# A new order and a new choice of engines for attention followed by a max-of-three feed-forward layer, on one Trainium2 core

## The chip, the core and the metric

The kernel runs on one core of one Trainium2 chip. Its engines are TensorE (PE in the profile; its weight loads are PEld), VectorE (DVE), ScalarE (ACT), GpSimd (POOL) and SyncE (SP). They run side by side, each through its own list of instructions in order, and wait for one another through semaphores. The metric is device time in microseconds: 200.65 us is the median of three runs before the change (200.58 to 200.71). The profile is of one execution with a span of 199.3 us.

## The reference

Batch 4, 8 heads, 768 positions, head size 64. Heads of one kind ("retrieval") see the whole past; the others see the first 4 positions and a window of 64. The attention output, 3072 rows of 512, goes through three projections whose elementwise maximum goes through a fourth.

```python
def _attn_ref(q, k, v, is_retrieval, n_sink, window):
    scores = scale * np.matmul(q, k.transpose(0, 1, 3, 2))
    stream_keep = causal & (is_sink | in_win)
    mask = np.where(retr[0, :, 0, 0, None, None], full_mask, stream_mask)
    scores = np.where(mask[None], scores, -1000000000.0)
    a = np.exp(scores - np.max(scores, axis=-1, keepdims=True))
    a = a / (np.sum(a, axis=-1, keepdims=True) + 1e-09)
    return np.matmul(a, v).astype(np.float32)

def _moe_ref(x, w1, w2, w3, w_out):          # x: 3072 x 512, w1..w3: 512 x 768, w_out: 768 x 512
    h = np.maximum(np.maximum(x @ w1, x @ w2), x @ w3)
    return (h @ w_out).astype(np.float32)
```

## The kernel before

The work is cut into 16 tasks t: batch (4), half of the sequence (2), group of four heads (2). A task has two pairs of heads, i = 0 and 1, and its scores come in units u: two for the first half of the sequence, four for the second. For each unit TensorE makes the scores in PSUM (`st`), ScalarE takes the exponential into `pt` in SBUF, and a mask is multiplied in place. That multiply is on GpSimd unless (t, i, u) stands in a list:

```python
    MASK_ON_DVE = ((2, 0, 1), (3, 0, 0), (3, 0, 1), (3, 1, 3), (5, 0, 0), (5, 1, 0), (5, 1, 1), (7, 0, 1))

    def masks(t, i, u):
        # ...
        for at, u0, nu, cols, n, m0 in APART if t in (3,) else MASKED[half]:
            # ... x: a part of pt, m: the mask of the two heads
            engine = nc.vector if (t, i, u) in MASK_ON_DVE else nc.gpsimd
            engine.tensor_tensor(out=x, in0=x, in1=m, op=ALU.mult)
```

`APART` cuts one 512-element mask of task 3 into two of 256 elements. In task 0 and 1 the masks are added in PSUM by TensorE instead (from `mk`, built by `head_masks`).

V is cast from fp32 to fp16 (`va`), and a second copy `vf` is multiplied by a flag for each head (zero where a head doesn't see far keys). The engine of each is an argument:

```python
    def prep_v(t, i, op, vf_engine):
        # ...
        op(out=vdst, in_=vs[:, hs])                        # the cast into va
        vf_engine.tensor_tensor(out=vf[...], in0=..., in1=far[...], op=ALU.mult)
```

`av(t, i)` multiplies `pt` with `va` and `vf` on TensorE (`oacc`); VectorE takes the reciprocal of the row sums (`rc`) and scales (`x`). `x` is transposed into `xT`, for tasks 0, 1 and 3 by TensorE (`turn_x`, written `x t i` in the table below), for the others by a DMA. When all four pairs of a half are there, the feed-forward `ffn` of that half joins a queue: 18 groups of four matmuls (`yy`), moved from PSUM by ScalarE (`acc`) and VectorE (the maximum, into `acc` and `hT`), and 6 output matmuls for each of three row blocks. `fill(n)` takes n steps from that queue, so that TensorE has work between scores.

Q and K of batch 0 come as fp32, are cast (`cast_pair`: `kn`, `qn`), transposed by TensorE (`turn_pair`) and copied to `KQ`. Those of batches 1 to 3 are loaded by a casting DMA of GpSimd's queue (`load`, tile `kq`) and transposed by VectorE (`turn`, a 32 x 32 STREAM_TRANSPOSE into `KQ`).

The opening is a hand-written sequence of such calls, the rest a table with a row for each unit of scores: the number of queue steps, whether the two pairs are apart, and four places for calls (ahead of the scores, after them, half-way through the queue steps, at the end). In it `v 2 0 ap` is `prep_v` for task 2, pair 0, cast on ScalarE (a), `vf` on GpSimd (p); d is VectorE.

```python
    cast_pair(0, 0, (act, act))
    idle_work(8)                 # matmuls on zeros
    read_flags()
    idle_work(2)
    head_flags()
    turn_pair(0, 0, dve, act)
    head_masks(0, True)
    cast_pair(0, 1, (pool, act))
    turn_pair(0, 1, dve)
    # ...
    FIRST = 4                    # units 0 to 3 (tasks 0 and 1) are in the opening
    PROGRAM = (
        (2.4, True, "", "", "cast 1 2 dp", ""),
        (2.4, False, "load 1 0", "", "cast 1 3 da", ""),
        # ... 45 more rows
    )
    for (units, apart, *lines), slot in itertools.zip_longest(PROGRAM, SLOTS[FIRST:]):
        run(lines[0])
        if slot and apart:
            scores(*slot, (0,)); part = int(due + units / 3); fill(part); due -= part; scores(*slot, (1,))
        elif slot:
            scores(*slot)
        run(lines[1])
        due += units
        part = int(due / 2); fill(part); due -= part
        run(lines[2])
        part = int(due); fill(part); due -= part
        run(lines[3])
```

PSUM's eight banks: four in the pool `bank` (feed-forward, `oacc`, transposes), and two buffers of two banks for scores.

Of the kernel before, what the change touches and what calls it, by code (L numbers as in the profile page):

```python
# [34 lines left out]
    [(0, 0, 1, (0,), 256, 256), (0, 0, 1, (384,), 128, 0), (1, 1, 1, (0,), 256, 0)],  # L35
    [(1, 0, 2, (384,), 128, 0), (2, 2, 1, (0, 384), 128, 128), (3, 3, 1, (0,), 256, 0)],
]

APART = [(0, 0, 1, (384,), 128, 0), (1, 1, 1, (384,), 128, 0)] + MASKED[1][1:]


def _where(half):
# [9 lines left out]
def kernel(  # L52
# [14 lines left out]
    nc = tc.nc  # L67
# [50 lines left out]
    cast = {}  # L118
# [16 lines left out]
    def cast_pair(half, hp, engines):  # L135
        cast[half, hp] = []
        for nm, src, op in zip(("kn", "qn"), staged.pop((half, hp)), engines):
            x = half16.tile([P, HB, 2, D], FP16, tag=nm, name=nm)
            op(out=x, in_=src.rearrange("p h j d -> p j h d"))  # L139
            cast[half, hp].append(x)  # L140
# [84 lines left out]
    def idle_work(n):  # L225
        sink = sps.tile([P, 2, 512], FP32, tag="st", name="st")
        for _ in range(n):
            nc.tensor.matmul(sink[:, 0, :], zero[:, 0:P], zero, start=True, stop=True)
# [41 lines left out]
    def read_flags():  # L270
        nc.vector.tensor_scalar(
            out=RT1, in0=ir32[:, 0 : 2 * H : 2], scalar1=0.0, scalar2=None,
            op0=ALU.not_equal,
        )

    def head_flags():
        flags = bank([P, H], FP32, "flags")
        nc.tensor.matmul(flags, base[0:1, 0:P], RT1, start=True, stop=True)
        nc.vector.tensor_copy(out=RT, in_=flags)
        nc.vector.tensor_scalar(  # L280
            out=least, in0=RT, scalar1=-1.0, scalar2=1.5, op0=ALU.mult, op1=ALU.add
        )
# [10 lines left out]
    def head_masks(hp, early=False):  # L293
        for h in (2 * hp, 2 * hp + 1):
            nc.vector.tensor_scalar(
                out=mk[:, h], in0=kept, scalar1=least[:, h : h + 1],
                scalar2=-30000.0 if early else None,
                op0=ALU.is_le if early else ALU.is_gt,
                **({"op1": ALU.mult} if early else {}),
            )  # L300
# [4 lines left out]
    def load_weight(wi):  # L305
        if wi < 3:
            nc.gpsimd.dma_start(
                out=w_t[wi],
                in_=(moe_w1, moe_w2, moe_w3)[wi].rearrange("(ks p) n -> p ks n", p=P),
            )  # L310
        else:
            nc.gpsimd.dma_start(
                out=woutt, in_=moe_w_out.rearrange("(ns p) m -> p ns m", p=P)
            )
# [62 lines left out]
    def fill(n):  # L377
        while n > 0 and queue:
            try:
                next(queue[0])  # L380
                n -= 1
            except StopIteration:
                queue.pop(0)
# [73 lines left out]
                masks(t, i, u)  # L457


    MASK_ON_DVE = ((2, 0, 1), (3, 0, 0), (3, 0, 1), (3, 1, 3), (5, 0, 0), (5, 1, 0), (5, 1, 1), (7, 0, 1))  # L460

    def masks(t, i, u):
        b, half, qd = where(t)
        pt = pts[t, i]
        h0 = 4 * qd + 2 * i
        for at, u0, nu, cols, n, m0 in APART if t in (3,) else MASKED[half]:
            if at != u:
                continue
            m = mk[:, h0 : h0 + 2, m0 : m0 + n]
            if nu == 1 and len(cols) == 1:  # L470
                x = pt[:, u0, :, cols[0] : cols[0] + n]
            elif nu == 2:
                x = pt[:, u0 : u0 + 2, :, cols[0] : cols[0] + n]
                m = m.unsqueeze(1).to_broadcast([P, 2, 2, n])
            else:
                x = pt[:, u0].rearrange("p h (c n) -> p h c n", n=n)[:, :, 0:4:3]
                m = m.unsqueeze(2).to_broadcast([P, 2, 2, n])
            engine = nc.vector if (t, i, u) in MASK_ON_DVE else nc.gpsimd
            engine.tensor_tensor(out=x, in0=x, in1=m, op=ALU.mult)  # L479
# [40 lines left out]
    def turn_x(t, i, op=None):  # L520
# [18 lines left out]
    cast_pair(0, 0, (act, act))  # L539
    idle_work(8)  # L540
    read_flags()
    idle_work(2)
    head_flags()
    turn_pair(0, 0, dve, act)
    head_masks(0, True)
    cast_pair(0, 1, (pool, act))
    turn_pair(0, 1, dve)
    cast_pair(0, 2, (pool, pool))
    scores(0, 0, (0,))
    scores(0, 1, (0,))  # L550
    head_masks(1, True)
    load_weight(0)
    scores(0, 0, (1,))
    far_flags()
    cast_pair(0, 3, (pool, pool))
    head_masks(3, True)
    head_masks(2, True)
    turn_pair(0, 2, dve)
    scores(0, 1, (1,))
    turn_pair(0, 3, dve)  # L560
    prep_v(0, 0, dve, nc.gpsimd)
    prep_v(1, 0, dve, nc.vector)
    load_pairs(1, 0, 2, (nc.gpsimd, nc.gpsimd))
    prep_v(1, 1, pool, nc.gpsimd)
    scores(1, 0, (0,))
    scores(1, 1, (0,))
    scores(1, 0, (1,))
    prep_v(0, 1, act, nc.vector)
    av(0, 0)
    scores(1, 1, (1,))  # L570
    av(1, 0)
# [1 line left out]
    turn_x(0, 0, act)  # L573
    av(1, 1)
    load_weight(1)
    turn_x(0, 1, act)
    head_masks(0)
    cast_pair(1, 1, (act, act))
    load_pairs(1, 2, 2, (nc.gpsimd, nc.gpsimd))
    load_weight(2)  # L580
    load_v(0, 1, (nc.gpsimd,) * HB)
    turn_x(1, 0, dve)
    turn_x(1, 1, dve)
    cast_pair(1, 0, (act, act))
    fill(4)
    head_masks(2)
    turn_pair(1, 1, dve)
    turn_pair(1, 0, dve)
    head_masks(3)
    load_weight(3)  # L590
    fill(1)
    fill(1)
    fill(1)
    head_masks(1)
# [5 lines left out]

    FIRST = 4
    PROGRAM = (
        (2.4, True, "", "", "cast 1 2 dp", ""),
        (2.4, False, "load 1 0", "", "cast 1 3 da", ""),
        (2.0, False, "", "pair 1 2", "load 1 1", ""),
        (2.2, False, "pair 1 3", "v 2 0 ap", "", "v 2 1 ap"),
        (2.2, False, "", "gate, load_v 1 0", "", ""),
        (1.6, True, "", "av 2 0", "", "turn 1 0 0 0"),
        (1.0, True, "turn 1 0 0 1", "", "av 2 1, turn 1 0 1 0", ""),
        (2.2, True, "turn 1 0 1 1, load_v 1 1", "", "v 3 1 pp, v 3 0 ap, x 2 0", "turn 1 1 0 0"),  # L610
        (3.6, False, "turn 1 1 0 1", "x 2 1", "turn 1 1 1 1, av 3 1", ""),
        (2.8, False, "v 4 0 pp, av 3 0", "turn 1 1 1 0", "v 4 1 ap", ""),
        (3.6, False, "x 3 0, x 3 1", "", "", ""),
        (3.6, False, "av 4 0", "", "x 4 0, v 5 1 pp", "x 4 1, v 5 0 ap"),
        (2.8, False, "", "", "av 4 1", "av 5 0, load 2 0, v 6 0 pp"),
        (3.6, False, "x 5 0", "load 2 1", "", "av 5 1"),
        (3.8, False, "", "x 5 1", "", ""),
        (2.8, False, "", "load_v 2 0", "turn 2 0 1 0", "v 6 1 ap"),
        (4.8, False, "turn 2 0 0 1", "", "turn 2 0 0 0", "av 6 0"),
        (4.2, False, "", "", "", "x 6 0, x 6 1, turn 2 0 1 1"),  # L620
        (3.4, False, "", "av 6 1", "turn 2 1 0 1", ""),
        (5.4, False, "load_v 2 1", "v 7 0 ap, turn 2 1 0 0", "turn 2 1 1 0", "v 7 1 ap"),
        (3.4, False, "", "turn 2 1 1 1", "v 8 0 ap, x 7 0", "av 7 0"),
        (3.8, False, "av 7 1", "", "", "v 8 1 pp"),
        (3.94, False, "x 7 1", "", "av 8 0", "v 9 0 ap, av 8 1"),
        (3.2, False, "", "x 8 0, x 8 1", "", ""),
        (3.94, False, "", "", "av 9 0, v 9 1 ap", "load 3 0"),
        (3.6, False, "", "x 9 0, load 3 1", "x 9 1", ""),
        (5.6, False, "v 10 0 ap, av 9 1", "v 10 1 ap", "", ""),
        (3.14, False, "", "load_v 3 0", "turn 3 0 1 0", ""),  # L630
        (3.6, False, "turn 3 0 0 1", "av 10 0", "turn 3 0 0 0", ""),
        (3.4, False, "", "x 10 0", "av 10 1", "turn 3 0 1 1"),
        (6.2, False, "", "", "turn 3 1 0 1", "v 11 0 ap"),
        (3.2, False, "load_v 3 1", "turn 3 1 0 0", "turn 3 1 1 0", ""),
        (3.2, False, "v 11 1 pp", "x 10 1, turn 3 1 1 1", "v 12 0 ap", "av 11 0, x 11 0"),
        (3.4, False, "", "av 11 1", "", "v 12 1 ap"),
        (5.0, False, "x 11 1", "", "av 12 0", "v 13 0 ap, av 12 1"),
        (3.2, False, "", "x 12 0, x 12 1", "", ""),
        (4.0, False, "", "", "av 13 0, v 13 1 pp", ""),
        (5.2, False, "", "x 13 0", "x 13 1", ""),  # L640
        (3.94, False, "v 14 0 ap, av 13 1", "v 14 1 ap", "", ""),
        (4.4, False, "", "", "", ""),
        (4.0, False, "", "av 14 0", "", ""),
        (3.2, False, "", "x 14 0", "av 14 1", ""),
        (3.2, False, "", "", "", "v 15 0 ap"),
        (4.6, False, "", "", "", ""),
        (3.94, False, "v 15 1 ap", "x 14 1", "", "av 15 0, x 15 0"),
        (3.94, False, "", "av 15 1", "", ""),
        (3.94, False, "x 15 1", "", "", ""),
    )  # L650
    ops = {"d": dve, "a": act, "p": pool}
    engines = {"d": nc.vector, "p": nc.gpsimd}
# [2 lines left out]
        av=lambda *a: av(*map(int, a)),  # L655
# [71 lines left out]
```

The softmax here doesn't subtract the row's maximum and nothing guards it: scores larger than these inputs give would overflow.

## Time and profile before

| what | value |
|---|---|
| time, median of 3 | 200.65 us |
| profiled span | 199.3 us |
| PE busy | 189.7 us, 95% |
| DVE busy | 122.5 us, 61% |
| ACT busy | 131.7 us, 66% |
| POOL busy | 123.3 us, 62% |
| DMA moved | 26.48 MB, mean 133 GB/s |

Busy time is the union of an engine's instructions; in the groups of instructions the last numbers are total, mean of one in ns, and the idle time of the engine just ahead of them with what ended it. Several instructions start before the one ahead has ended by the record, so busy time in a short stretch can be less than the sum of durations. DMA is a share of 16 engines and passes 1 where records overlap. The chain is followed back from the last instruction through whatever released each step. Numbers of lines in a profile, L479 and so on, are those of the kernel's file.

### The profile page before, as it was taken

The page shows a single profiled execution, that of the slowest core. Times are in us where ns is not written, and L with a number is a line of the kernel's source. Part 1 is how long each engine was busy: PE and PEld are TensorE (multiplying, and loading weights), DVE is VectorE, ACT ScalarE, POOL GpSimd, SP SyncE. Part 2 cuts the span into 40 slices and gives each one's busy share as a digit, 9 for nine tenths or more (in the row PEclk, how much of TensorE's full clock was granted, in tenths as well). Part 3 has the DMA queues.
Part 4 walks back from the last instruction along what each step waited for, and adds up shares of the span by engine and source line. Part 5 has one row for each costly group of instructions (what it writes and reads, how often), then busy time and mean ns, then how long its engine had stood idle before and what let it go on. Part 6 is the DMA issues. An engine that isn't in the chain of part 4 may idle for free.

```text
span 199.3 us, 5133 instructions
## 1 busy us (share of the span) xinstructions
PE 189.7 (95%) x2059; PEld 109.5 (55%) x2059; DVE 122.5 (61%) x241; ACT 131.7 (66%) x206; POOL 123.3 (62%) x154
## 2 busy tenths in 40 slices
PE   7897999996999999999999999999999999999992
PEld 2455555545566465574555565565555565755652
DVE  2698587999687829861555649961555234543540
ACT  4585798786966776676786775848758769323221
POOL 3599159789887906787969635799847447400000
PEclk9999999999999999999999999999999999999999
DMA  6999999994949991904359995513410250023004
GB/s 182 270 213 245 278 238 212 213 202 112 256 81 154 194 274 43 178 0 146 95 101 132 170 254 141 85 26 98 116 23 20 105 76 20 3 64 135 3 0 158
DMA packets 43245, 26.48 MB, mean 133 GB/s; under 512 B 33558, under 2 KB 38230, under 8 KB 43222
## 3 DMA queue, kind: packets, MB, share of 16 engines
q1 hardware_dynamic: 37206, 15.01, 34.9%
q0 software_dynamic: 4784, 10.23, 26.7%
q10 hardware_dynamic: 1232, 0.92, 1.5%
q8 instruction: 16, 0.26, 0.6%
q14 instruction: 7, 0.06, 0.1%
HBM read 25.17 MB, written 6.29 MB: 158 GB/s over the span
## 4 chain that ended last, share of the span: by engine, by line
PE 78%; DVE 8%; ACT 4%; DMA 3%; issue 3%; POOL 2%; SPq 1%; ACTq 0%; POOLq 0%; DVEq 0%
PE yy L338 43%; PE yy L364 12%; PE st L441 10%; PE oacc L495 8%; DVE KQ L190 4%; PE yst L338 3%; ACT pt L452 3%; DMA ks<-in_k_dram 2%; DVE x L505 2%; DMA out_dram<-ot 1%; PE tr L157 1%; PE yst L364 1%; POOL kn L139 1%; DVE hT L349 1%; POOL qn L139 0%
## 5 line engine op out<-in xcount | busy, mean ns | idle before, releaser
L479 POOL TENSOR_TENSOR pt<-pt,mk 128x512 f16<-128x512 f16 (+1 forms) x76 | 80.6, 1084 | 34.8 <-ACT pt L452 34.7
L452 ACT ACTIVATE pt<-st 128x1024 f16<-128x1024 f32 (+3 forms) x99 | 83.1, 894 | 19.4 <-PE st L441 18.6
L349 DVE TENSOR_TENSOR acc<-yy,acc 128x384 f16<-128x384 f32 x45 | 25.1, 558 | 28.9 <-PE yy L338 19.3
L338 PE MATMUL yy<-xT,w1t 128*128 128x384 f16 x180 | 36.1, 327 | 0.1
L338 PE MATMUL yy<-xT,w0t 128*128 128x384 f16 x180 | 35.6, 326 | 0.4 <-DVE xT L531 0.4
L338 PE MATMUL yy<-xT,w2t 128*128 128x384 f16 x180 | 35.7, 327 | 0.0
L346 ACT CAST acc<-yy 128x384 f16<-128x384 f32 x45 | 21.0, 485 | 17.0 <-PE yy L338 10.5
L364 PE MATMUL yy<-woutt,hT 128*128 128x512 f16 (+1 forms) x138 | 32.0, 375 | 0.0
L441 PE MATMUL st<-KQ 32*128 32x384 f16 (+4 forms) x560 | 28.7, 279 | 1.0 <-DVE KQ L190 0.8
L349 DVE TENSOR_TENSOR hT<-yy,acc 128x384 f16<-128x384 f32 x45 | 25.1, 560 | 6.6 <-PE yy L338 4.0
L495 PEld LDWEIGHTS <-pt 128*128 128x128 f16 x672 | 24.0, 97 | 5.3 <-issue 2.1
L190 DVE STREAM_TRANSPOSE KQ<-kq 128x384 f32<-128x384 f32 x24 | 25.7, 1130 | 0.0
L338 PEld LDWEIGHTS <-w0t 128*128 128x128 f16 x192 | 18.2, 98 | 12.9 <-issue 1.0
L495 PE MATMUL oacc<-va,pt 128*128 128x65 f16 x352 | 24.8, 193 | 0.3 <-ACT va L392 0.3
L338 PEld LDWEIGHTS <-w2t 128*128 128x128 f16 x192 | 17.6, 98 | 13.3 <-issue 2.1
L338 PEld LDWEIGHTS <-w1t 128*128 128x128 f16 x192 | 17.2, 98 | 12.8 <-issue 1.3
L370 ACT COPY ot<-yy 128x512 f32<-128x512 f32 x22 | 12.9, 588 | 15.9 <-PE yy L364 9.6
L364 PEld LDWEIGHTS <-hT 128*128 128x128 f16 x150 | 14.0, 98 | 14.6 <-issue 0.3
L441 PEld LDWEIGHTS <-KQ 32*128 32x128 f16 (+1 forms) x560 | 12.2, 93 | 17.8 <-issue 11.5
L495 PE MATMUL oacc<-vf,pt 128*128 128x65 f16 x320 | 21.2, 193 | 0.8 <-POOL vf L394 0.8
L505 DVE TENSOR_TENSOR x<-oacc,rc 128x384 f16<-128x384 f32 x32 | 17.8, 557 | 1.1
L503 DVE RECIPROCAL rc<-oacc 128x6 f32<-128x6 f32 x32 | 6.1, 192 | 20.0 <-PE oacc L495 19.8
(70 smaller groups left out, 129.9 us busy)
## 6 DMA issues: line engine op xcount, KB each, us to landing
out_dram<-ot SPq DMA_DIRECT2D x23, 256.0 KB, 3.1
vs<-in_v_dram SPq DMA_DIRECT2D x21, 256.0 KB, 6.3
kq<-in_k_dram POOLq DMA_DIRECT2D x6, 384.0 KB, 5.6
kq<-in_q_dram POOLq DMA_DIRECT2D x6, 384.0 KB, 8.0
qs<-in_q_dram ACTq DMA_DIRECT2D x4, 192.0 KB, 4.0
ks<-in_k_dram SPq DMA_DIRECT2D x4, 192.0 KB, 3.6
w0t<-in_moe_w_dram POOLq DMA_DIRECT2D x1, 768.0 KB, 7.4
ks<-in_k_dram POOLq DMA_DIRECT2D x2, 384.0 KB, 7.2
```

The source lines that it names most:

```text
L190: nc.vector.transpose(out=dst.rearrange("c (p j) -> c j p", j=n)[:, j0:j1], in_=src.rearrange("c (j i) -> c j i", i=R),)
L338: nc.tensor.matmul(yy[:, 0:HALF], w_t[wi][:, ks, ni * P : (ni + 1) * P], xT[b, half][ks].rearrange("p a t -> p (a t)"), start=(ks == 0), s ...
L346: nc.scalar.copy(out=acc[ni], in_=yy[:, 0:HALF])
L349: nc.vector.tensor_tensor(out=dst, in0=yy[:, 0:HALF], in1=acc[ni], op=ALU.max)
L364: nc.tensor.matmul(yo[:, 0:n], hT[ns][:, tb * P : (tb + 1) * P], woutt[:, ns, c : c + n], start=(ns == 0), stop=(ns == NNB - 1),)
L370: op(out=ot[:, c : c + n], in_=yo[:, 0:n])
L441: nc.tensor.matmul(sts[g // m][:, g % m, c0 : c0 + n * P], KQ[rows, 0, ki * P : (ki + 1) * P], KQ[rows, 1, t0 : t0 + n * P], start=(c0 == ...
L452: nc.scalar.activation(out=pts[t, i][:, u, h0 : h0 + m, 0:w], in_=st[:, :, 0:w], func=AF.Exp, scale=sc,)
L479: engine.tensor_tensor(out=x, in0=x, in1=m, op=ALU.mult)
L495: nc.tensor.matmul(o[:, qi, hl, 0 : D + 1], pt[:, u, hl, c : c + P], vv[:, 2 * hp + hl, ki, 0 : D + 1], start=(idx == 0), stop=(idx == len ...
L503: nc.vector.reciprocal(out=rc, in_=o[:, :, :, D])
L505: nc.vector.tensor_tensor(out=x, in0=o[:, :, :, 0:D], in1=rc.unsqueeze(3).to_broadcast([P, HB, 2, D]), op=ALU.mult,)
```

## The change

The table and the opening's order were set anew by an offline search, together with the engines that do the masks and the V casts. Its stated aim is to keep VectorE's casts from running beside GpSimd's work. The computation is the same. `APART` goes; the list of masks on VectorE goes from 8 entries to 14, without (3, 0, 0). Cut to the core:

```diff
-APART = [(0, 0, 1, (384,), 128, 0), (1, 1, 1, (384,), 128, 0)] + MASKED[1][1:]
-    MASK_ON_DVE = ((2, 0, 1), (3, 0, 0), (3, 0, 1), (3, 1, 3), (5, 0, 0), (5, 1, 0), (5, 1, 1), (7, 0, 1))
+    MASK_ON_DVE = ((2, 0, 1), (2, 0, 3), (3, 0, 1), (3, 1, 3), (5, 0, 0), (5, 1, 0), (5, 1, 1), (7, 0, 1), (9, 0, 0), (11, 0, 1), (11, 0, 2), (13, 0, 0), (15, 0, 1), (15, 0, 2))
-        for at, u0, nu, cols, n, m0 in APART if t in (3,) else MASKED[half]:
+        for at, u0, nu, cols, n, m0 in MASKED[half]:
     read_flags()
+    head_flags()
+    cast_pair(0, 1, (pool, act))
     idle_work(2)
-    head_flags()
+    head_masks(0, True)
     turn_pair(0, 0, dve, act)
-    head_masks(0, True)
-    cast_pair(0, 1, (pool, act))
     turn_pair(0, 1, dve)
 # ... cut
     turn_pair(0, 2, dve)
+    turn_pair(0, 3, dve)
     scores(0, 1, (1,))
-    turn_pair(0, 3, dve)
 # ... cut
     turn_x(0, 1, act)
-    head_masks(0)
     cast_pair(1, 1, (act, act))
 # ... cut
     fill(4)
+    head_masks(0)
     head_masks(2)
 # ... cut: the table's first rows
-        (2.4, True, "", "", "cast 1 2 dp", ""),
-        (2.4, False, "load 1 0", "", "cast 1 3 da", ""),
-        (2.0, False, "", "pair 1 2", "load 1 1", ""),
+        (2.4, True, "", "cast 1 2 dp", "", ""),
+        (2.4, False, "load 1 0", "", "cast 1 3 da", "load 1 1"),
+        (2.0, False, "", "", "", "pair 1 2"),
         (2.2, False, "pair 1 3", "v 2 0 ap", "", "v 2 1 ap"),
-        (2.2, False, "", "gate, load_v 1 0", "", ""),
+        (2.2, True, "", "gate, load_v 1 0", "", ""),
         (1.6, True, "", "av 2 0", "", "turn 1 0 0 0"),
-        (1.0, True, "turn 1 0 0 1", "", "av 2 1, turn 1 0 1 0", ""),
+        (1.0, False, "turn 1 0 0 1", "av 2 1", "turn 1 0 1 0", ""),
-        (2.2, True, "turn 1 0 1 1, load_v 1 1", "", "v 3 1 pp, v 3 0 ap, x 2 0", "turn 1 1 0 0"),
-        (3.6, False, "turn 1 1 0 1", "x 2 1", "turn 1 1 1 1, av 3 1", ""),
-        (2.8, False, "v 4 0 pp, av 3 0", "turn 1 1 1 0", "v 4 1 ap", ""),
+        (2.2, True, "turn 1 0 1 1, load_v 1 1", "", "v 3 1 pp, v 3 0 ap, x 2 0", ""),
+        (3.6, False, "turn 1 1 0 0, turn 1 1 0 1", "x 2 1", "turn 1 1 1 1, av 3 1", ""),
+        (2.8, False, "av 3 0", "turn 1 1 1 0", "v 4 0 pp", "v 4 1 pp"),
 # ... cut: later rows are moved in the same way; V casts of (4,1), (7,1) and (15,0) go from
 # ... ScalarE to GpSimd, and the vf multiply of (6,0) goes from GpSimd to VectorE
```

## The prediction

> **What bounds the kernel now.** I read the page's busy slices first, then busy time cut into five stages of my own choosing, then TensorE's waits before 50 us and after it, then the chain and the timelines of the places where TensorE stood still. The slices (40 of 5 us, tenths of busy time):
>
> ```profile
> PE   7897999996999999999999999999999999999992
> DVE  2698587999687829861555649961555234543540
> POOL 3599159789887906787969635799847447400000
> DMA  6999999994949991904359995513410250023004
> ```
>
> TensorE (PE) has four weak places: the first four slices, the tenth, and the last. DMA is full from 5 to 45 us. The stages put numbers to that (columns: stage, its length, then busy us and instruction count of PE, PEld, DVE, ACT, POOL):
>
> ```profile
> 0.00:18.70 18.70, 15.27 (x146) 8.27 (x147) 13.30 (x40) 11.10 (x21) 13.20 (x28) 1.00 1.02 229
> 18.70:43.30 24.60, 24.38 (x227) 13.30 (x227) 20.25 (x36) 20.50 (x31) 16.37 (x20) 1.00 1.12 231
> 43.30:50.10 6.80, 4.60 (x109) 3.12 (x108) 6.51 (x12) 4.43 (x8) 6.72 (x9) 1.00 0.52 122
> 50.10:193.10 143.00, 142.90 (x1567) 83.24 (x1564) 82.02 (x154) 94.09 (x145) 87.00 (x100) 1.00 0.52 104
> 193.10:199.30 6.20, 2.59 (x18) 1.57 (x16) 0.42 (x1) 1.54 (x3) 0.00 (x0) 0.92 0.35 127
> ```
>
> PE idles 18.70 - 15.27 = 3.4 us in the opening, 0.2 in the next stage, 6.80 - 4.60 = 2.2 around 43 to 50, 0.1 in the long stage, and the tail has no work for it. So all that any reordering can win is about 3.4 + 0.2 + 2.2 + 0.1 = 6 us (3%), and 5.6 of it lies before 50 us. After 50 us the list of PE's waits is empty; before 50 us it has these (engine and line, what ended the wait, us in total, times, longest):
>
> ```profile
> PE tr L527 <- DVE x L505: 1.2, 3, 0.6
> PE st L441 <- DVE KQ L190: 0.8, 2, 0.5
> PE oacc L495 <- POOL vf L394: 0.8, 1, 0.8
> PE tr L157 <- ACT qn L139: 0.7, 1, 0.7
> ```
>
> Two things stand behind them. One is the input DMA, which fills both early stages: the answer on the weight w1t shows its weight load waiting for the landing,
>
> ```profile
>   DMA w1t<-in_moe_w_dram: 0.4, 1
> ```
>
> and PE goes on at 23.39, where w1t landed at 23.34. The other shows in the chain, where VectorE's work follows without a break (start, us, what):
>
> ```profile
> 43.92 0.25 DVE pt L479
> 44.17 2.94 DVE KQ L190 x3
> ...
> 48.42 1.05 DVE KQ L190
> ```
>
> PE's scores of the next head group start at 49.51, right behind this. By the trace the four loads that these KQ transposes read landed at 39.07, 40.91, 43.02 and 45.07, and the transposes began at 39.23, 41.84, 44.10 and (the third of three) about 46.05. So the DVE run of 39 to 49.5 us is tied to arrivals, with slack of 0.2 to 1.1 us.
>
> [...]A mask multiply of 256 elements on DVE took 2.31 us while GpSimd ran a row of instructions without a gap:
>
> ```profile
> 34.90 2.31 DVE L479 TENSOR_TENSOR pt<-pt,mk 128x256 f16<-128x256 f16 x1 [0.83 <-ACT pt L452]
> 33.22 2.28 POOL L479 TENSOR_TENSOR pt<-pt,mk 128x512 f16<-128x512 f16 x2
> 35.44 1.61 POOL L394 TENSOR_TENSOR vf<-va,far 128x384 f16<-128x384 f16 x2
> 37.01 1.46 POOL L479 TENSOR_TENSOR pt<-pt,mk 128x256 f16<-128x256 f16 x2
> ```
>
> It ended at 37.21, just after the two vf multiplies; twice the size took 0.42 at 27.58 with GpSimd idle. [...]Here a 512-element mask is 1160 ns on POOL in the mean and 424 unhindered on DVE, 2.7 times. [...]while GpSimd's queue drains, from 20 to 36 us, nothing of SyncE's data queue moves and the DMA share stays above 1. [...]the repeated matmul step of 163 ns for 384 columns I take as unchanged, since no matmul changes.
>
> **The change, part by part.** PE's list keeps its 2059 matmuls. The order of the built programs differs in a handful of places, and runs of equal kind go from 163 to 162. So PE's own work is the same to a tenth of a microsecond.
>
> *Opening.* The head flags move ahead of two of ten dummy matmuls (about 0.43 us each from 4.45 us for ten), so flags come 2 x 0.43 = 0.9 us earlier, and the first masks with them. ScalarE casts qn of pair 1 ahead of its KQ copy, so that PE's wait for it (0.7 us at 7.55) should go. But the next thing PE needs from GpSimd, qn of pair 3, follows the load of pair 2 (landed at 7.07) through kn 0.6, qn 0.5, issue of w0t 0.9, vf 0.7, kn 0.6, qn 0.5: 7.12 + 3.8 = 10.9 us against 11.44 now, since only the 0.64 us wait for far goes. The transposes of pair 3 now stand before a scores step of 0.55 us, so PE comes out of this at about 11.65 us, where it is at 11.67 now. Later, two mask builds (0.9 us, 17.43 to 18.34) leave the place in front of the two xT copies that PE waited for until 18.66. Worth 0.6 us there, to about 18.0. Then PE reaches w1t at 22.4 instead of 23.0 us, but w1t lands when the full DMA queue gets to it. GpSimd issues the same loads in the same order and the first one (w0t, 8.13) hangs on the same arrival, so I keep 23.3. Of the 0.6, 0 to 0.3 remains.
>
> *23 to 50 us.* The mask of (3,0,0), the one that took 2.31 us, goes to GpSimd with the split masks undone: t = 3 has one 512-element mask in place of two of 256. DVE takes (2,0,3) instead, at 32 to 33 us, when GpSimd is also at work; it can be blocked as the old one was, in the worst case until about 35.9 us. Without a block DVE is some 1.3 us earlier at 38 us. Then comes the KQ transpose, which can't begin before 39.07 us, and it begins at 39.23 already: 0.1 us is left of the 1.3. The next hold is the mask (3,1,3), which waits for an exponential that ends at 43.36 and for GpSimd's mask until 43.70; it starts at 43.72 now. From there the DVE order is the same as before (three KQ, two rc and x, one KQ: 44.1 to 49.46). I give this stage 0.1 us, plus or minus 0.3.
>
> *After 50 us.* DVE's masks go from 10 to 18. Counted by form, GpSimd loses 6 of 512 and 4 of 256 elements (6 x 1.16 + 4 x 0.68 = 9.7 us) and one vf multiply (0.8), and gets three V casts from ScalarE (3 x 0.585 = 1.8): 123.3 falls to about 114.6 us. DVE gains 8 masks of 512 elements at 0.42 to 0.59 (3.4 to 4.7 us) and the vf multiply, for about 127 us; ScalarE loses 3 x 0.516 = 1.5. None of it is on the path: PE is 142.90 of 143.00 us busy here, so lightening GpSimd buys at most 0.1 us. It can only cost: each new DVE mask can sit behind a 1.16 us GpSimd instruction and hold up the max operations that free PSUM banks. Four banks at 0.65 us a group of matmuls cover about 2.6 us of that, so I expect few stalls: 0 to 0.5 us in all.
>
> *Tail.* The av of the last half stands 8 matmuls (1.3 us) later, before the last 18 output matmuls. Its DMA transpose landed at 178.56 and was first needed near 180.6, so some 0.7 us of slack remains. No change.
>
> Sum: -0.15 (opening) -0.1 (23 to 50) -0.1 + 0.25 (after 50) is -0.1; and as the order was searched for with time as its aim, I lean to -0.4: 200.2 us.
>
> **The rivals.** (a) *The first 50 us are not tied to the loads as I think*: w1t lands earlier because its neighbours are issued about half a microsecond earlier. For it: PE's waits there add up to 5.6 us. Against it: DMA at 9 tenths in every slice from 5 to 45 us. It would give 198.5 to 199.5. (b) *VectorE becomes the bound after 50 us*, because its masks in order block behind GpSimd. For it: the 2.31 us above, and single masks of 1.24 and 0.99 us at 51.84 and 54.73. Against it: those did not stop PE, and DVE is only 57% busy (82.02 of 143.00). It would give 201 to 202.5. (c) *The block moves to (2,0,3)* at 32 us, and the five maxima behind it delay PE by 1 us or more. Then 0 to 1 us is lost near 36 us, partly hidden in the idle time of 43 to 50: 200.5 to 201.
>
> **Range and chances.** Half the weight on the sum near 200.2, a quarter on (a), the rest on (b) and (c). 8 in 10: 199.0 to 201.6. The 2% bound needs 4.0 us, two thirds of all idle time or a new stall as long as all that exists: 3% faster, 2% slower.
>
> **What would show it.** Right: PE's wait for qn gone; PE still going on at w1t's landing near 23.3; the scores at 49.5 now within 0.4 us of there; PE 99% busy from then on; POOL near 114.6 and DVE near 127 us. Wrong: w1t landing before 22.9; scores at under 48.5; or a stage after 50 us with more than 0.5 us of PE idle time behind DVE. What would break the prediction most is a PE stall that repeats in each of the four batches.

## The result and the profile after

The changed kernel takes 201.79 us (median of 4 runs, 201.44 to 202.44). The old one, beside it on the same chip, takes 200.68 us (200.58 to 200.72). The ratio is 1.006, with an interval of 1.0032 to 1.0088: slower by about 1.1 us, inside 2%, and just above the range of 199.0 to 201.6.

The profiled execution of the changed kernel has a span of 200.7 us. Its busy slices, with the clock granted to TensorE:

```profile
PE   7798996996899999999999999999999999999992
DVE  2888879699778847882655649973455245443540
POOL 3699178169996824977769604598737523700000
PEclk9999999699999999999999999999999999999998
DMA  5999999998519992623469994502401240024004
```

PE has a new weak place in slice 7 (30 to 35 us, 6 tenths), where the old row had a nine. In slice 8 it is busy, but the granted clock falls to 6 tenths. From slice 12 on PE is full, as it was. The five stages, cut at the same times as in the prediction and with the same columns:

```profile
0.00:18.70 18.70, 15.22 (x150) 8.25 (x151) 13.69 (x41) 11.94 (x24) 13.81 (x29) 1.00 1.02 235
18.70:43.30 24.60, 22.73 (x216) 12.83 (x214) 20.55 (x35) 18.04 (x26) 12.46 (x16) 0.93 1.13 234
43.30:50.10 6.80, 5.26 (x95) 3.09 (x93) 6.41 (x11) 5.16 (x9) 6.72 (x8) 1.00 0.82 180
50.10:193.10 143.00, 142.47 (x1579) 83.27 (x1579) 85.46 (x165) 94.20 (x144) 81.46 (x96) 1.00 0.49 100
193.10:200.70 7.60, 4.06 (x25) 2.24 (x23) 1.16 (x3) 1.54 (x3) 0.00 (x0) 0.90 0.29 104
```

The loss is in the second stage: PE idles 24.60 - 22.73 = 1.9 us there, where it idled 0.2, and does 216 instructions instead of 227. The 0.5 us of idle time in the fourth stage is not new: the second of the two gaps that stood just ahead of 50.1 us (0.6 and 0.5 us) has slid past that cut, because everything is later.

Times of the same events place it more exactly than fixed cuts. "Half clock" below is a stretch in which the granted clock is one half:

| event, us | before | after |
|---|---|---|
| first matmul with w1t | 23.39 | 22.15 |
| scores of the second head group of batch 1 (the point at 49.5 in the prediction) | 49.51 | 51.14 |
| last matmul ends | 195.69 | 197.16 |
| first to second | 26.12 | 28.99 |
| second to third | 146.18 | 146.02 |

So 2.87 us are lost between 22 and 51 us, and nothing is lost after that. PE's waits before 50 us of the changed kernel name the place (engine and line, what ended the wait, us in total, times, longest):

```profile
PE yy L336 <- DVE hT L347: 1.8, 1, 1.8
...
PE tr L155 <- POOL kn L137: 1.3, 2, 0.7
```

The first line is new: the feed-forward matmuls waited once, for 1.8 us, for a maximum on VectorE that frees their bank. The wait for qn from ScalarE is gone, as meant, but PE now waits 1.3 us for kn from GpSimd instead. The timelines of VectorE, GpSimd and PE around the new wait show what held the maxima (start, length, engine, line, operation, tiles):

```profile
29.58 1.81 DVE L160 COPY KQ<-tr 128x768 f16<-128x768 f16 x2
31.31 3.47 DVE L477 TENSOR_TENSOR pt<-pt,mk 128x512 f16<-128x512 f16 x1
34.71 2.59 DVE L347 TENSOR_TENSOR hT<-yy,acc 128x384 f16<-128x384 f32 x5
29.54 3.40 POOL L477 TENSOR_TENSOR pt<-pt,mk 128x512 f16<-128x512 f16 x3
32.88 1.61 POOL L392 TENSOR_TENSOR vf<-va,far 128x384 f16<-128x384 f16 x2
35.30 1.40 PE L336 MATMUL yy<-xT,w2t 128*128 128x384 f16 x4 [1.77 <-DVE hT L347]
```

The mask of (2,0,3), new on VectorE, took 3.47 us instead of about 0.42. GpSimd ran five instructions in a row, three masks and two vf multiplies, until 32.88 + 1.61 = 34.49 us; the VectorE mask began in the middle of the row and ended at 34.78, 0.3 us after the row's last instruction. Five maxima stood behind it, PE ran out of free banks and stood still for 1.77 us. Right after that the granted clock was 0.50 for 3.41 us (35.38 to 38.79): the four matmuls of the last line took 1.40 us, where four equal ones took 0.82 just before the stop.

The run of VectorE's work that fed the scores at 49.5 us stands in the new chain in the same order, 1.3 to 1.6 us later, and the lines ahead of it show what it hangs on (start, us, what):

```profile
42.45 1.42 PE yy L362 x6
...
44.47 0.72 ACT pt L450
45.21 0.58 DVE pt L477
45.79 2.95 DVE KQ L188 x3
...
50.05 1.04 DVE KQ L188
```

The mask (3,1,3) at 45.21 waits for an exponential, and that one for PE and ScalarE's work before it. No load stands in this part of the chain.

### The profile page after: what moved, and what is told of

Same layout as the page of the kernel before. It is cut to its first block, busy times and chain, and to the rows that moved or that the text cites. A ratio compares the mean times of both kernels' runs of the same rounds, so it can differ in the third digit from the quotient of the medians.

```text
span 200.7 us, 5122 instructions
## 1 busy us (share of the span) xinstructions
PE 189.7 (95%) x2059; PEld 109.7 (55%) x2059; DVE 127.3 (63%) x250; ACT 130.9 (65%) x203; POOL 114.5 (57%) x146
## 4 chain that ended last, share of the span: by engine, by line
PE 83%; DVE 6%; DMA 3%; issue 2%; ACT 2%; POOL 1%; SPq 0%; DVEq 0%; ACTq 0%
PE yy L336 44%; PE yy L362 13%; PE st L439 11%; PE oacc L493 10%; PE yst L336 3%; DMA ks<-in_k_dram 2%; DVE KQ L188 2%; DVE x L503 1%; PE st L423 1%; DVE KQ L160 1%; ACT pt L450 1%; DMA out_dram<-ot 1%; PE tr L155 1%; PE yst L362 1%; ACT ot L368 1%
## 5 line engine op out<-in xcount | busy, mean ns | idle before, releaser
L477 POOL TENSOR_TENSOR pt<-pt,mk 128x512 f16<-128x512 f16 x66 | 70.9, 1095 | 46.6 <-ACT pt L450 30.8
L336 PE MATMUL yy<-xT,w2t 128*128 128x384 f16 x180 | 36.5, 331 | 1.8 <-DVE hT L347 1.8
L493 PEld LDWEIGHTS <-pt 128*128 128x128 f16 x672 | 24.6, 98 | 5.7 <-issue 1.6
L493 PE MATMUL oacc<-va,pt 128*128 128x65 f16 x352 | 25.5, 194 | 0.2 <-ACT pt L450 0.2
L477 DVE TENSOR_TENSOR pt<-pt,mk 128x512 f16<-128x512 f16 (+1 forms) x18 | 11.7, 673 | 19.0 <-ACT pt L450 19.0
L493 PE MATMUL oacc<-vf,pt 128*128 128x65 f16 x320 | 21.7, 195 | 0.9 <-POOL vf L392 0.9
```

What stands on the lines that cost most here:

```text
L336: nc.tensor.matmul(yy[:, 0:HALF], w_t[wi][:, ks, ni * P : (ni + 1) * P], xT[b, half][ks].rearrange("p a t -> p (a t)"), start=(ks == 0), s ...
L493: nc.tensor.matmul(o[:, qi, hl, 0 : D + 1], pt[:, u, hl, c : c + P], vv[:, 2 * hp + hl, ki, 0 : D + 1], start=(idx == 0), stop=(idx == len ...
```

## The experiments

Three theories. **A**: the block on (2,0,3) is the loss. **B**: the six further masks that go to VectorE (tasks 9 to 15) hold up PE's banks later. **C**, formed after the first runs: the block needs the new table as well, because the table moves a DMA issue on GpSimd. The experiments ran on other chips than the result above, beside the old kernel at 201.0 us, so I compare ratios. The letters in the quoted expectations are these; where an expectation splits A, it says how. "The seventh experiment" in them is number 6 below.

**1. The mask (2,0,3) back on GpSimd.** After, with one entry out of the list:

```diff
-    MASK_ON_DVE = ((2, 0, 1), (2, 0, 3), (3, 0, 1), (3, 1, 3), ...
+    MASK_ON_DVE = ((2, 0, 1), (3, 0, 1), (3, 1, 3), ...
```

> The changed kernel with one entry taken out of the list of VectorE's masks: (2, 0, 3) is on GpSimd again. Theory A (the loss is that mask: 3.47 us on VectorE behind GpSimd's run of masks and vf multiplies, five maxima behind it, TensorE stopped for 1.9 us near 33 us): TensorE has no wait for hT, reaches the scores of (3,1) about 1.9 us sooner than in the changed kernel, the scores of the second head group of batch 1 at 48.5 to 49.3 instead of 51.14, and the time is 199.2 to 200.0. Theory B (the loss is in the further VectorE masks and the new rows after 50 us): time stays at 201.3 to 202.0.

Measured: 200.24 us, ratio 0.9962 (0.9944 to 0.9981). The wait for hT is gone. One entry of the list turns the change from 0.6% slower to 0.4% faster. The scores of batch 1 come at 50.25 us in this trace, later than expected, because PE began with w1t only at 24.43; the stretch between the two is 25.82 us, where the changed kernel needs 28.99.

**2. The same mask on VectorE, behind the maxima.** After, with (2,0,3) still on VectorE, but issued later, at the end of its row of the table:

```diff
-            if not early:
+            if not early and (t, i, u) != (2, 0, 3):
...
-        (2.2, True, "", "gate, load_v 1 0", "", ""),
+        (2.2, True, "", "gate, load_v 1 0", "", "m 2 0 3"),       # m: masks(t, i, u)
```

> The changed kernel with the mask (2, 0, 3) still on VectorE, but placed in the program after the last of the five maxima (hT) of that stage and ahead of the av of task 2. Theory A: what hurts is the place of the mask in VectorE's order, not the engine; it runs near 35 us, when GpSimd is idle, takes 0.42 us, TensorE does not stop; 199.2 to 200.0. Theory B: 201.3 to 202.0. If the engine's load as such were at fault: 201 or more.

Measured: 200.15 us, 0.995 (0.9925 to 0.9974). The mask in VectorE's timeline:

```profile
35.64 0.41 DVE L477 TENSOR_TENSOR pt<-pt,mk 128x512 f16<-128x512 f16 x1
```

It starts after GpSimd's row (which ends at 35.43 here) and takes 0.41 us. VectorE has the same work as in the changed kernel and the loss is gone. So it is the place of the mask that costs, not the load on the engine.

**3. The new opening alone.** Before, with only the opening's order of the change (the calls moved as in the diff above; table and lists old). Cut to the moves of most weight:

```diff
+    head_masks(0, True)
     turn_pair(0, 0, dve, act)
-    head_masks(0, True)
...
+    turn_pair(0, 3, dve)
     scores(0, 1, (1,))
-    turn_pair(0, 3, dve)
...
-    head_masks(0)
     cast_pair(1, 1, (act, act))
...
+    head_masks(0)
     head_masks(2)
```

> The kernel before with the new opening alone (its table, its masks and its casts as before). Theory A: the opening is worth 1.2 us where the second weight is first used (near 22.1 instead of 23.39), w1t lands near 22 instead of 23.3, and some of it, 0.5 to 1.2 us, is kept to the end: 199.4 to 200.2. Rival, that of my prediction (the full DMA queue holds w1t at 23.3 and the gain is lost): 200.4 to 200.8.

Measured: 200.98 us, 1.0007 (0.9987 to 1.0028). The opening is worth nothing at the end.

**4. Without the further masks on VectorE.** After, with the six entries of tasks 9 to 15 back on GpSimd:

```diff
-    ..., (7, 0, 1), (9, 0, 0), (11, 0, 1), (11, 0, 2), (13, 0, 0), (15, 0, 1), (15, 0, 2))
+    ..., (7, 0, 1))
```

> The changed kernel without the six further VectorE masks of tasks 9 to 15 (they are on GpSimd again), but with (2, 0, 3). Theory A: nothing changes, 201.3 to 202.3, the stop of TensorE near 33 us is there as before. Theory B: the time falls to 200.0 to 200.7.

Measured: 202.06 us, 1.0042 (1.0019 to 1.0064): the loss stays, with the same stop of 1.77 us. From the scores of batch 1 to the last matmul it takes 146.04 us, the changed kernel 146.02. B falls: these masks cost nothing and bring nothing.

**5. A shorter row on GpSimd.** After, leaving out the two vf multiplies of task 2; its `av` reads `va` in their place, so two multiplies of 0.8 us are not done and the far keys of that task are not cut off.

```diff
+        if t == 2:
+            return                              # ahead of the vf multiply in prep_v
-            vv = va[j] if half * HB + qi - ki < 2 else vf[j]
+            vv = va[j] if half * HB + qi - ki < 2 or t == 2 else vf[j]
```

> The changed kernel, leaving out the two vf multiplies of task 2 on GpSimd (its av reads va in place of vf, so that heads with a window see the far keys of task 2; TensorE's work is the same). Theory A1 (the VectorE mask (2, 0, 3) is shut out for as long as GpSimd's instructions follow one another without a gap): the mask ends at about the end of GpSimd's third mask, near 33 us, and takes some 1.7 us instead of 3.47; TensorE's wait for hT shrinks from 1.8 us to 0.3 or less, and the time is 0.994 to 1.001 of the kernel before. Rival A2 (something else holds VectorE until about 34.7, such as a late exponential or the loads): the mask keeps its 3.4 us, and the time is 1.004 or more.

Measured: 200.11 us, 0.9963 (0.9944 to 0.9983). The mask and GpSimd's row in the timelines of this run:

```profile
31.88 1.89 DVE L479 TENSOR_TENSOR pt<-pt,mk 128x512 f16<-128x512 f16 x1
30.10 3.38 POOL L479 TENSOR_TENSOR pt<-pt,mk 128x512 f16<-128x512 f16 x3
```

The row now ends at 33.48 and the mask at 33.77, again 0.3 us behind it. Cutting 1.61 us off the row shortens the block by 3.47 - 1.89 = 1.58 us, and PE waits 0.2 us in place of 1.8. In both traces the block is what was left of the row when the mask began (3.18 and 1.60 us) plus 0.3 us.

**6. The entry alone, in the old kernel.** Before, with (2,0,3) added to its list:

```diff
-    MASK_ON_DVE = ((2, 0, 1), (3, 0, 0), ...
+    MASK_ON_DVE = ((2, 0, 1), (2, 0, 3), (3, 0, 0), ...
```

> The kernel before with one entry added to the list of VectorE's masks: (2, 0, 3). Theory A: the one entry is enough; VectorE's mask is shut out for 2 us or more near 33 us also in the old table, the maxima behind it come late, TensorE stops for 0.5 us or more near 35 us, and the time is 1.003 to 1.012 of the kernel before. If the harm needs the new table as well: 0.998 to 1.002.

Measured: 200.53 us, 0.998 (0.9966 to 0.9993). A loss was expected and none came: A in its simple form, that the entry suffices, falls. The timelines of VectorE and GpSimd say why:

```profile
31.70 0.42 DVE L479 TENSOR_TENSOR pt<-pt,mk 128x512 f16<-128x512 f16 x1
31.63 0.59 POOL L174 DMA_DIRECT2D kq<-in_k_dram  x1
32.22 0.54 POOL L174 DMA_DIRECT2D kq<-in_q_dram  x1
```

In the old table GpSimd issues the two loads of `load 1 1` just when VectorE comes to this mask, and the mask runs unhindered in 0.42 us beside the issue. In the changed kernel the same two issues stand at 28.41 and 28.99 us, ahead of the row of five. That is theory C.

**7. A gap made by a memset.** After, with a GpSimd instruction that reads nothing put into its row, behind the mask (2,1,2):

```diff
+            if (t, i, u) == (2, 1, 2):
+                nc.gpsimd.memset(gap, 0.0)       # 512 elements of scratch
```

> The changed kernel with one more instruction: a memset of a scratch tile (512 elements, some 0.5 us) on GpSimd between its masks (2, 1, 2) and (2, 1, 3). Theory A1a (VectorE gets its turn as soon as GpSimd does something that reads nothing in SBUF): the VectorE mask ends at about 32.5 us and takes 1.0 to 1.3 us instead of 3.47, TensorE does not stop, time 0.994 to 1.000 of the kernel before. A1b (any instruction of GpSimd in a run keeps VectorE out): the mask takes 3.9 to 4.1 us, and the time is 1.006 to 1.012.

Measured: 203.29 us, 1.0102 (1.0069 to 1.0135). It makes no gap; the block grows from 3.47 to 3.92 us, by 0.45, and the memset takes 0.54:

```profile
31.82 3.92 DVE L478 TENSOR_TENSOR pt<-pt,mk 128x512 f16<-128x512 f16 x1
32.25 0.54 POOL L480 MEMSET gap<- 128x512 f16 x1
```

GpSimd goes on with a mask and two vf multiplies until 35.46 us, and VectorE's mask ends at 35.74. PE's wait for hT is 2.2 us here, against 1.8.

**8. The DMA issue back in its place.** After, with `load 1 1` again one row later; VectorE's order is that of the changed kernel, instruction for instruction:

```diff
-        (2.4, False, "load 1 0", "", "cast 1 3 da", "load 1 1"),
-        (2.0, False, "", "", "", "pair 1 2"),
+        (2.4, False, "load 1 0", "", "cast 1 3 da", ""),
+        (2.0, False, "", "", "load 1 1", "pair 1 2"),
```

> The changed kernel with one call of the table put back to where it was: load 1 1 (two DMA issues of GpSimd, some 1.1 us) stands after the scores of (2,2) again instead of one row sooner; all masks and their engines are those of the changed kernel. Theory C (after the seventh experiment: the harm is the pair, the mask (2, 0, 3) on VectorE and the DMA issues moved out of GpSimd's run, which left no place where VectorE gets in): the mask runs while GpSimd issues those DMAs, in 0.42 to 0.8 us, TensorE does not stop, 0.993 to 0.998 of the kernel before. If another part of the new table brings the block: the mask keeps 2 us or more, 1.003 or more.

Measured: 199.89 us, 0.993 (0.9904 to 0.9956). The mask on VectorE and the first of the two issues on GpSimd, from the timelines:

```profile
32.08 0.42 DVE L477 TENSOR_TENSOR pt<-pt,mk 128x512 f16<-128x512 f16 x1
31.60 0.59 POOL L172 DMA_DIRECT2D kq<-in_k_dram  x1
```

Moving one call by one row takes the whole loss away and leaves a gain of 0.7%. The order of PE, VectorE and ScalarE is untouched, and the two loads land at 40.77 and 42.83 us, where in the changed kernel they land at 40.69 and 42.82. So it is the pause in GpSimd's row that counts, not the arrival of the data.

**9. Both halves of the cause in the old kernel.** Experiment 6, with `load 1 1` one row sooner as in the new table; VectorE's order is that of experiment 6:

```diff
-        (2.4, False, "load 1 0", "", "cast 1 3 da", ""),
-        (2.0, False, "", "pair 1 2", "load 1 1", ""),
+        (2.4, False, "load 1 0", "", "cast 1 3 da", "load 1 1"),
+        (2.0, False, "", "pair 1 2", "", ""),
```

> The kernel before with the pair alone: (2, 0, 3) on VectorE and load 1 1 one row sooner. Theory C: now the mask is shut out in the old table too, for 2 us or more near 32 us, TensorE waits for hT for 0.5 us or more, and the time is 1.003 to 1.012 of the kernel before (0.998 with the mask alone in the seventh experiment). If the pair is not enough: 0.996 to 1.001.

Measured: 202.52 us, 1.0066 (1.0028 to 1.0104), with the changed kernel's block, here in the timelines of VectorE, GpSimd and PE:

```profile
32.33 3.88 DVE L479 TENSOR_TENSOR pt<-pt,mk 128x512 f16<-128x512 f16 x1
30.98 3.39 POOL L479 TENSOR_TENSOR pt<-pt,mk 128x512 f16<-128x512 f16 x3
34.32 1.61 POOL L394 TENSOR_TENSOR vf<-va,far 128x384 f16<-128x384 f16 x2
36.74 0.81 PE L338 MATMUL yy<-xT,w2t 128*128 128x384 f16 x4 [1.77 <-DVE hT L349]
```

PE stops for 1.77 us, and the stretch from the first w1t matmul to the scores of batch 1 grows from 25.81 (experiment 6) to 27.48 us, by 1.67. Almost nothing later hides the stop. There is no half clock in this trace (mean granted clock 1.0), so these 1.67 us are the stop alone. The old order, with nothing of the change but the entry and the earlier issue, is as slow as the changed kernel.

**10. The old block taken away.** Before, without (3,0,0) on VectorE, the mask that had taken 2.31 us:

```diff
-    MASK_ON_DVE = ((2, 0, 1), (3, 0, 0), (3, 0, 1), ...
+    MASK_ON_DVE = ((2, 0, 1), (3, 0, 1), ...
```

> The kernel before without (3, 0, 0) in the list of VectorE's masks: that half mask, which took 2.31 us behind GpSimd, goes to GpSimd. If the 0.4 to 0.5% by which the first two experiments are under the kernel before come from the end of that block: the DVE stretch from 35 to 38 us is 1.5 us or more shorter, and the time is 0.995 to 0.998. If they come from the rest of the new table: 0.999 to 1.001.

Measured: 201.44 us, 1.0013 (0.9998 to 1.0029). No gain, though VectorE comes through that place sooner: its next mask begins at 36.04 us in place of 38.06, of which 0.8 us is an earlier start with w1t in this execution; that leaves 1.2 us, where 1.5 or more was asked for. PE's waits keep their kind (0.9 us for vf, 0.7 for x, 0.5 for KQ). The block of the old kernel, which the change removes, was off the path.

**11. A combined version.** After, with experiment 2, the mask (3,1,3) on GpSimd, and the V casts of task 3 two rows earlier, both on ScalarE:

```diff
-        (1.6, True, "", "av 2 0", "", "turn 1 0 0 0"),
+        (1.6, True, "", "av 2 0", "v 3 1 ap, v 3 0 ap", "turn 1 0 0 0"),
...
-        (2.2, True, "turn 1 0 1 1, load_v 1 1", "", "v 3 1 pp, v 3 0 ap, x 2 0", ""),
+        (2.2, True, "turn 1 0 1 1, load_v 1 1", "", "x 2 0", ""),
```

> A version meant to beat both: the changed kernel with (2, 0, 3) late on VectorE as in the second experiment, the V work of task 3 two rows earlier (casts on ScalarE, vf on GpSimd, both idle then), and the mask (3, 1, 3) on GpSimd, so that VectorE's run of KQ transposes does not wait for the exponential before it. Theory A: the scores of the second head group of batch 1 start near 48.3 us (49.1 in the second experiment), time 0.988 to 0.994 of the kernel before. If GpSimd's longer run of masks (4.5 us) holds up the av of task 3: 0.994 to 0.998.

Measured: 199.79 us, 0.9935 (0.991 to 0.9959). In VectorE's timeline five transposes now follow one another without a break where the mask had cut them into two and three:

```profile
40.51 4.94 DVE L188 STREAM_TRANSPOSE KQ<-kq 128x384 f32<-128x384 f32 x5
```

The scores of batch 1 start at 48.38 us (49.06 in experiment 2). Of the 0.68 us, 0.25 is an earlier start with w1t in this execution (22.85 against 23.10), so 0.43 is left. VectorE saves more, the mask and the wait of 0.31 us for the exponential ahead of it, but gives part back: PE has a new wait of 0.5 us for that mask, now on GpSimd.

**12. The combined version with the old place of one call.** Experiment 11, with `scores(0, 1, (1,))` ahead of `turn_pair(0, 3, dve)` again, as in the old opening:

```diff
-    turn_pair(0, 3, dve)
     scores(0, 1, (1,))
+    turn_pair(0, 3, dve)
```

> The combined version (0.9935 of the kernel before) with the two lines of the opening in their old order: the scores of (0, 1) for the second pair ahead of the transposes of pair 3, so that TensorE has work while it waits for kn. It spares up to 0.6 us at 10.3 us. If the opening is held by the loads (w1t landing near 22.3 to 22.8), the gain is lost and the time is as for the combined version, 0.992 to 0.995; if not, 0.990 to 0.992.

Measured: 199.51 us, 0.9927 (0.9902 to 0.9953): faster than both kernels, and not told apart from experiments 8 and 11 by these intervals. PE's wait for kn at this place is gone, but w1t landed at 22.53 us, and the time is in the range named for a lost gain.

## Why the prediction was wrong

**The cause, shown.** Two moves of the new table meet. The mask (2,0,3) goes to VectorE, and the issue of `load 1 1`, the pause in GpSimd's row in which VectorE could have run it, goes away. Either alone is harmless (the entry in experiments 6 and 8, the earlier issue in experiment 1), the two together stop PE for 1.77 us in the new order and in the old (experiment 9).

**The step that failed** is "23 to 50 us", with its "0.1 us, plus or minus 0.3". It named the block, "in the worst case until about 35.9 us" (it lasted until 34.78), and then left it out of the sum; it cost a stop of 1.77 us. Three things in it were wrong.

- *Whether the block would come.* I judged this from the engines being busy at the same time, not from GpSimd's own order. The diff shows `load 1 1` moving a row; the prediction doesn't take up that this moves 1.1 us in which GpSimd runs no mask. For the later masks it counted on a block by one GpSimd instruction ("behind a 1.16 us GpSimd instruction"), which was my estimate. Its own lines show more: the mask that began at 34.90 and ended at 37.21 outlasted the GpSimd mask then running, which ended at 35.49, and two vf multiplies as well, which ended at 37.05.
- *Whether it would be hidden.* Rival (c) is what happened, and its size was put at 0 to 1 us, "partly hidden in the idle time of 43 to 50". Almost nothing of it was hidden. PE's idle time there stands behind VectorE's transposes, these behind the mask (3,1,3), and this behind an exponential of scores that PE itself must make. So a delay of PE at 33 us moves the idle time along: 1.77 us of stop became 1.67 us at 50 us in experiment 9.
- *What the run of VectorE hangs on.* "Tied to arrivals" rested on loads that landed at 39.07 to 45.07 us in one execution. In the thirteen other traces, four of them with the old table or one row off it, the first of these loads landed between 36.82 and 38.44 us. In the changed kernel it landed at 36.82 and its transpose began at 39.95, three microseconds later. The near coincidence of landing and start in the old profile was chance.

**The sum again, with the measured terms.** In the traces, the stretch to the scores of batch 1 is 28.99 us in the changed kernel and 25.81 in experiment 8, where only the block is missing. Of the 3.18 us, 1.77 are the stop; the remaining 1.4 us goes with the half clock (a granted clock of 0.50 for 3.41 us). In experiment 7 the two executions with a mean granted clock of 0.989 and 0.990 have spans of 201.7 and 202.2 us, the two with 0.998 and 1.0 of 200.4 and 201.2; experiment 9, with 1.0, loses nothing beyond its stop (1.67 us for 1.77). The times contain less of it: the mean granted clock was 0.988 in one of the changed kernel's four executions, the slowest, and 0.998 or more in the others, so the median of 201.79 holds the stop and hardly the half clock. Without the block the new order is faster than the old by 0.4 to 0.7% (experiments 1, 2 and 8), 0.8 to 1.4 us. With the stop, that makes 1.8 - 0.8 to 1.4 = 0.4 to 1.0 us of loss, and 1.1 was measured, which fits within the intervals.

**What was right.** PE's own work stayed at 189.7 us. After 50 us nothing changed: 146.18 us before, 146.02 after, so the lean to a small cost there was not needed and rival (b) did not come. POOL came to 114.5 us (114.6 predicted) and DVE to 127.3 (about 127). The opening's gain does not reach the end (experiment 3). The step there said that w1t would keep 23.3; single traces scatter more than the step allowed: w1t landed between 22.23 and 23.34 in four traces with the old opening, and between 21.97 (the changed kernel) and 23.86 (experiment 1) in nine with the new one. So its sign of being wrong, w1t before 22.9, says little: it came with the old opening as well. Rival (a), that the first 50 us are less tied to the loads than I thought, was right about the stretch after 23 us: experiment 11, with five transposes in one run, takes 25.53 us from w1t to the scores of batch 1, and the old kernel 26.12.

**Two readings that were wrong without consequence.** The idle time before 50 us is 3.4 + 0.2 + 2.2 = 5.8 us, not 5.6. And that nothing of SyncE's queue moved from 20 to 36 us does not show that GpSimd's queue held it up: SyncE issued nothing between 7.8 and 35.8 us. No run here tests that.

**What stays open.** Of the 1.4 us that experiment 8 gains on the old kernel, the traces place 0.31 us (26.12 - 25.81) before the scores of batch 1 and 0.15 us (146.18 - 146.03) after them. Another 0.47 us (23.39 - 22.92) lies before the first w1t matmul, where one trace against one does not settle it, since experiment 3 gives the opening alone nothing. The remaining 0.5 us is not in these two traces.

## What to carry to other kernels

When a VectorE multiply of two tiles in SBUF, such as these masks, is moved, look at what GpSimd runs in that very place: a row without a pause can cost VectorE the rest of the row (1.89 to 3.92 us here for a mask of 0.42), so put the multiply behind the work that others wait for (0.41 us in experiment 2), or beside GpSimd's DMA issues (0.42 us in experiments 6 and 8). Then ask what frees the banks of TensorE behind it. Idle time later on TensorE's list is no cushion where the wait that makes it hangs on TensorE's own earlier results: 1.77 us of stop was still 1.67 us at the scores of batch 1 (experiment 9).

## What the runs showed of the hardware

**A row, not one instruction.** In the four traces of such a block shown above, the VectorE mask (2,0,3) took 1.89, 3.47, 3.88 and 3.92 us, against 0.41 to 0.42 in experiments 2, 6 and 8. It did not end with one of the single GpSimd masks (1.15 us each) but 0.3 us after the last instruction of the row. The memset of experiment 7 (0.54 us) did not end the block of the mask that had already begun; a mask that starts beside a memset is in no run here. Beside GpSimd's two DMA issues (0.59 and 0.54 us) the mask took 0.42 us, in experiments 6 and 8. But a row doesn't always count as one. The old kernel's mask of 34.90 us ended at 37.21, 0.16 us after the two vf multiplies, though GpSimd's masks went on until 38.47, and in the changed kernel a VectorE mask ended at 57.47, 0.27 us after a single GpSimd mask, with a cast next in the row (start, length and line from VectorE's and GpSimd's timelines):

```profile
56.48 0.99 DVE L477 TENSOR_TENSOR pt<-pt,mk 128x512 f16<-128x512 f16 x1 [0.40 <-ACT pt L450]
56.04 1.16 POOL L477 TENSOR_TENSOR pt<-pt,mk 128x512 f16<-128x512 f16 x1 [0.40 <-ACT pt L450]
57.14 0.70 POOL L390 CAST va<-vs 128x384 f16<-128x384 f32 x1
```

Why the VectorE mask ends behind one GpSimd instruction in some places and behind the whole row in others is open.

**Half clock behind a short stop.** In the changed kernel the granted clock was 0.50 from 35.38 to 38.79 us, 3.41 us long, behind a stop of TensorE of only 1.77 us (33.53 to 35.30). In experiment 7 the stop was 2.23 us, until 36.27; eight matmuls for scores then took 1.03 us at 37.01, where eight equal ones took 0.61 at 32.67, and the mean granted clock of that execution was 0.989. After an equal stop of 1.77 us in experiment 9 the mean granted clock was 1.0, and the profiled execution of experiment 1, without the wait for hT, had 0.988. The mean granted clock was 0.991 or less in 6 of 34 executions of the kernels with the stop, and in 9 of 247 of the others. So the stop alone does not decide, and why the half clock came in these executions is not settled.
